# Second-layer gate logits with stationary weights in column groups, and the clears of a row buffer issued earlier

## The chip, the cores and the metric

One NeuronCore of one Trainium2 chip. The time is that of one execution on the device, in microseconds (us): 507.88 us, median of 3 runs (507.73 to 507.91). The page and the trace come from one more execution under the profiler.

## The reference

An attention over 4 batches of 512 tokens with 32 state rows each (8 heads of 64) gives 2176 rows of 512 features. Two mixture-of-experts layers follow, each with 8 experts, one expert for each row:

```python
logits = x @ w_gate                      # [2176, 512] @ [512, 8], fp32
expert_idx = np.argmax(logits, axis=1)
gate_w = softmax(logits)[n, expert_idx]
h = np.maximum(x_e @ w1[e], 0.0)         # 512 -> 1024
out = gate_w * (h @ w2[e])               # 1024 -> 512
```

The first layer has a capacity for each expert, the second has none. The argmax needs the logits in full fp32, so their product runs as fp32 matmuls, which stand in the trace as two weight loads and two matmuls each.

## The kernel before

All stages are written into one program with an order laid out by hand; each engine runs its own instructions in that order.

**Attention and first routing.** Four slots, one for a batch, write the 2176 rows to `xrows` in DRAM (a row is 512 features and its gate weight, 513 floats). The route of a batch takes the argmax, counts rows for each expert, and writes the gate weights with small DMAs of SP (`route`, L667, L668). Then lists of row numbers are made for each expert (`enlist_batch`).

**Layers.** Rows of one expert are worked in groups of 512 (four tiles of 128, the "quad"), gathered by indirect DMAs of GpSimd (L580). `stage` runs one group and `tail` its end together with the beginning of the next. `m1_quad` (L1056) does the first product of a chunk of 128 hidden features, 12 matmuls of 128x512, then ACT makes the rounded ReLU `hTh` (L1064) and DVE the rest `hTl` (L1065). `m2_quad` (L1068) does the second product: four tiles, three matmuls each. `ORDER` interleaves them. After every 3 or 4 matmuls the program calls a `Part`, which counts events 0, 1, 2, ... of the stage: at an event number other work is placed, such as casts of weight chunks, turns of tiles and logits. Weights come as raw fp32 chunks of 512 KB over SP's queue (`wload`, L273); ACT casts the high part (L277, L1291) and GpSimd or DVE subtracts for the low part (L278, L1292). `tail` turns the next group's four gathered tiles (`x_quad`, L1036, by `turn`, L1029): four transposes on TensorE, an ACT cast and a DVE subtraction each, in banks `ph[0]`, `pyT`, `ph[1]`, `pyT`. Small remainders of experts run beside groups (`small`, `one`).

**Gate logits of layer 2.** The finished rows of a layer 1 group lie in `ysb`. During the next group (and during the first group of layer 2 for the last rows) `Logits` makes their logits: `turn` (L1116) transposes a tile into bank `pyT` and ACT copies it to `yT` or to the scratch `hs`; `product` (L1120) multiplies, with the turned tile as stationary weights and the 512x8 gate matrix `wg2p` moving, 8 columns; DVE copies the 128x8 result (L1124). Four, six and six tiles are done in this run's three groups that have logits. `TURNS` and `TURNS0` give the event of each turn and each product. When the last product is done, `behind` (L1142) goes on: argmax on DVE, one-hot counts on TensorE (L1157 to L1161), places, gates and the store of the rows into `yrows` by indirect DMAs (L1091).

**The row buffer.** `yrows`, the input of layer 2, is cleared by four DMAs from a row of zeros (`fills`, L706 to L711). They are a step in the background queue `bgq`: generators of which each event of the first group takes up to four steps (`tick`, L103; `TQ = 4`). The queue is filled at L1529, behind what is left of the route of batch 1. The first group's stage begins at about 83 us; the loads of the second group's weights are placed at its event 22 (`planned`, L1503) and issued when the number of groups is known.

Of the kernel before, what the change touches and what calls it, by code (L numbers as in the profile page):

```python
# [10 lines left out]
F32 = mybir.dt.float32  # L11
# [8 lines left out]
P = 128  # L20
B, H, S, D = 4, 8, 512, 64
NS = 32
DM = H * D
E = 8
# [39 lines left out]
PLANNED, READY, GET = ((22, 29), 35, 0)  # L64
QUICK = (4, 3)
GAP = 2
TURNS0 = ((0, 1), (1, 3), (4, 5), (5, 6), (6, 7), (7, 8))
ON = ((1, 1, 1, 1), (1, 1, 1, 1), (0, 1, 0, 1), (0, 0, 0), (1, 1, 1, 1))
TURNS = ((6, 7), (7, 8), (8, 10), (11, 12), (12, 13), (13, 14))
ALL = (ET.Pool, ET.Activation, ET.PE, ET.DVE, ET.SP)  # L70
WHY = "the value is a count worked out on the chip within these bounds"

# [2 lines left out]
def moe_kernel(ctx: ExitStack, tc: tile.TileContext, x, state, wg1, w1a, w2a, cap, wg2, w1b, w2b, out):  # L75
# [17 lines left out]
    def ctile(shape, dt, name):  # L93
        return cp.tile(shape, dt, name=name)
# [5 lines left out]
    bgq = deque()  # L100
# [14 lines left out]
    def named(name, g):  # L115
        yield from g
        done.add(name)
# [9 lines left out]
    def abreast(*gs):  # L127


        gs = [[g, -1] for g in gs]  # L130
        while gs:
            n = 0
            for s in list(gs):
                if s[1] == clock[0]:
                    continue
                n += 1
                try:
                    if next(s[0]) is PAUSE:
                        s[1] = clock[0]
                    else:  # L140
                        yield
                except StopIteration:
                    gs.remove(s)
            if not n:
                yield PAUSE
# [10 lines left out]
    SP.dma_start(out=wg1_sb, in_=wg1.rearrange("(c p) e -> p c e", p=P))  # L156
    wg1h = ctile([D, H, E], F32, "wg1h")
    SP.dma_start(out=wg1h, in_=wg1.rearrange("(h d) e -> d h e", d=D))
    wg2p = ctile([P, NC1, E], F32, "wg2p")
    cap_i = ctile([P, 2], I32, "cap_i")  # L160


    zb = ctile([P, 4 * P], BF16, "zb")
    DVE.memset(zb, 0.0)
    ident = ctile([P, P], F32, "ident")
# [461 lines left out]
    def route(b0, nb, then=(), quick=False):  # L627

        n, run = nb * (R + 1), runs_[0]
        lg = lgs[:, b0:b0 + nb].rearrange("p b r e -> p (b r) e")  # L630
        gt = gts[:, b0:b0 + nb].rearrange("p b r -> p (b r)")
        ohb = rtp.tile([P, nb, R + 1, E], BF16, tag="oh", name="oh")
        oh = ohb.rearrange("p b r e -> p (b r) e")
        mv = []
        yield from argmax_onehot(rtp, lg, n, smask[:, 0:nb].rearrange("p b r -> p (b r)"), oh, mv)
        m, v = mv
        cs = rtp.tile([P, nb, R, E], BF16, tag="cs", name="cs")
        rs = rtp.tile([P, nb, 2, E], BF16, tag="rs2", name="rs2")
        DVE.tensor_copy(rs[:, :, 1], ohb[:, :, R])
        DVE.tensor_copy(cs[:, :, 1], ohb[:, :, 0])  # L640
        yield
        for r in range(2, R):
            DVE.tensor_tensor(out=cs[:, :, r], in0=cs[:, :, r - 1], in1=ohb[:, :, r - 1], op=ALU.add)
            yield
        DVE.tensor_tensor(out=rs[:, :, 0], in0=cs[:, :, R - 1], in1=ohb[:, :, R - 1], op=ALU.add)
        yield
        yield from pauses(QUICK[0]) if quick else idle(IDLE[0])
        w = nb * 2 * E
        rsv = rs.rearrange("p b a e -> p (b a e)")
        PE.matmul(pyv[:, 0:w], upper, rsv, start=True, stop=True)  # L650
        PE.matmul(pyv[:, w:2 * w], ones, rsv, start=True, stop=True)
        prs = rtp.tile([P, 2, nb, 2, E], F32, tag="prs", name="prs")
        DVE.tensor_copy(prs.rearrange("p t b a e -> p (t b a e)"), pyv[:, 0:2 * w])
        yield
        preb = rtp.tile([P, nb, R + 1, E], F32, tag="pre", name="pre")
        pre = preb.rearrange("p b r e -> p (b r) e")
        for i in range(nb):
            for a, r in ((0, 0), (1, R)):
                DVE.tensor_tensor(out=preb[:, i, r], in0=run, in1=prs[:, 0, i, a], op=ALU.add)
                DVE.tensor_tensor(out=run, in0=run, in1=prs[:, 1, i, a], op=ALU.add)  # L660
                yield
        yield from then

        def gates():
            yield from gate_of(rtp, lg, m, n, gt)
            for b in range(b0, b0 + nb):
                SP.dma_start(out=xrows[b * ST:b * ST + S, DM:ROW].rearrange("(p r) o -> p r o", p=P), in_=gts[:, b, 0:R, None])  # L667
                SP.dma_start(out=xrows[b * ST + S:(b + 1) * ST, DM:ROW], in_=gts[0:NS, b, R:R + 1])  # L668

        res = []  # L670

        def places():
            DVE.tensor_tensor(out=preb[:, :, 1:R], in0=cs[:, :, 1:R], in1=bc(preb[:, :, 0:1], [P, nb, R - 1, E]), op=ALU.add)
            yield
            far = rtp.tile([P, n, E], F32, tag="far", name="far")
            DVE.tensor_tensor(out=far, in0=pre, in1=bc(cape[:, None, :], [P, n, E]), op=ALU.is_ge)
            yield
            DVE.scalar_tensor_tensor(out=pre, in0=far, scalar=FAR, in1=pre, op0=ALU.mult, op1=ALU.add)
            yield
            yield from slots(rtp, oh, v, pre, n, res)  # L680

        yield from abreast(places(), gates())
        for i in range(nb):
            pp_[b0 + i] = [t[:, i * (R + 1):(i + 1) * (R + 1)] for t in res]
# [3 lines left out]
    def enlist_batch(b, quick=False, eng=(DVE, DVE, POOL)):  # L688

        pp, ek = pp_[b]  # L690
        todo = []
        for r in range(R + 1):
            np_ = P if r < R else NS
            oc = lsp.tile([P, NK], BF16, tag="loc", name="loc")
            ov = lsp.tile([P, 2, P], BF16, tag="lov", name="lov")
            yield from enlist(oc, ov, eng, np_, pp[:, r:r + 1], ek[:, r:r + 1], tida[:, b, r:r + 1], tidb[:, b, r:r + 1], todo)
            if len(todo) > LAG[b]:
                enlist_mm(*todo.pop(0))
        yield from pauses(QUICK[1]) if quick else idle(IDLE[1])
        while todo:  # L700
            enlist_mm(*todo.pop(0))
            yield from () if quick else idle(IDLE[2])
# [3 lines left out]
    def fills(*parts):  # L706

        g = NTOK // P
        for i in parts:
            lo, hi = g * i // 4, g * (i + 1) // 4  # L710
            SP.dma_start(out=yrows.rearrange("(g p) w -> p g w", p=P)[:, lo:hi], in_=bc(zeros[:, None, :], [P, hi - lo, ROW]))  # L711
        yield
# [16 lines left out]
    with ExitStack() as ac:  # L729
# [13 lines left out]
        xload(1, 2)  # L743
        xload(2, 2)
        SP.dma_start(out=cap_i, in_=bc(cap.bitcast(I32).rearrange("(o c) -> o c", o=1), [P, 2]))
        SP.dma_start(out=wg2p, in_=wg2.rearrange("(c p) e -> p c e", p=P))

        sd = ap_.tile([P, B, NH, P], F32, name="sd")
        vg = ap_.tile([P, B, NH, GW], F32, name="vg")
# [259 lines left out]
    hTh = wk2.tile([P, 2, QT * P], F32R, name="hTh")  # L1009
    hTl = wk2.tile([P, 2, QT * P], F32R, name="hTl")  # L1010
    hTf = wk2.tile([P, NC2, P], F32, name="hTf")
    hs = wk2.tile([P, 512], F32, name="hs")
    yT = [wk2.tile([P, NC1, P], F32, name="yT"), hs.rearrange("p (c t) -> p c t", c=NC1)]
    gq = [wk2.tile([P, QT], F32, name=f"gq{i}") for i in range(3)]
    g1 = wk2.tile([P, 1], F32, name="g1")
    gy = wk2.tile([P, QT + 2], F32, name="gy")
# [12 lines left out]
    def turn(bank, src):  # L1029

        for c in range(NC1):
            PE.transpose(bank[:, c * P:(c + 1) * P], src[:, c * P:(c + 1) * P], ident)
        return bank.rearrange("p (c t) -> p c t", c=NC1)
# [76 lines left out]
    class Logits:  # L1110

        def __init__(self, n, y0):
            self.n, self.y0, self.done = n, y0, 0
            self.lg = Sized(n).tile([P, n, E], F32, "lg", "lg2")

        def turn(self, i):  # L1116
            if i < self.n:
                ACT.copy(yT[i % 2].rearrange("p c t -> p (c t)"), turn(pyv, ysb[:, self.y0 + i]).rearrange("p c t -> p (c t)"))

        def product(self, i, bank):  # L1120
            if i < self.n:
                for c in range(NC1):
                    PE.matmul(bank[:, 0:E], yT[i % 2][:, c], wg2p[:, c], start=(c == 0), stop=(c == NC1 - 1))
                DVE.tensor_copy(self.lg[:, i], bank[:, 0:E])  # L1124
                self.done += 1

        def events(self, turns):

            ev = []
            for i, (t, p) in enumerate(turns):  # L1130
                c = (p + 2) // 7
                bank = ph[(c + 1) % 2] if (p + 2) % 7 < 4 else pyv
                ev += [(p, lambda i=i, bank=bank: self.product(i, bank)), (t, lambda i=i: self.turn(i))]
            return ev

        def alone(self):
            for i in range(self.n):
                self.turn(i)
                self.product(i, pyv)
            return self  # L1140

# [384 lines left out]
    POOL.memset(meta, 0.0)  # L1526
    POOL.memset(ysb[:, 0], 0.0)
    POOL.memset(ysb[:, NY - 2:NY], 0.0)
    bgq += [abreast(route(2, 2, (), True), enlist_batch(1, True)), fills(0, 1, 2, 3), abreast(plan_runs(rp, 0), named("lists", chain(enlist_batch(2, True), enlist_batch(3, True)))), plan_lists(rp, 0)]  # L1529
    for t in range(QT):  # L1530
        x_quad(t, ysb[:, 1 + t], py[t], gq[0])
    st = stage(0, 0, [(PLANNED[0], lambda: planned(0)), (READY, room)], TQ)
# [53 lines left out]
```

## Time and profile before

| | us |
|---|---|
| median of 3 runs (range) | 507.88 (507.73 to 507.91) |
| profiled execution, its own time | 511.39 |
| span in the trace, first to last instruction | 509.5 |
| TensorE busy | 445.8 (87%) |
| TensorE weight loads busy | 326.0 (64%) |
| VectorE (DVE) busy | 195.2 (38%) |
| ScalarE (ACT) busy | 165.9 (33%) |
| GpSimd (POOL) busy | 216.5 (42%) |
| mean granted TensorE clock | 0.948 |

Busy times are of the profiled execution. [...] In rows of the timeline the first two numbers are start and duration in us, then engine, line, operation, output and inputs, shapes and count; in brackets stands how long the engine was idle before and what released it. "PEld" is the weight loading of TensorE, "SPq" the DMA issuing of SP. Matmuls overlap, so the distance from one start to the next says more than a duration.

### The profile page before, as it was taken

The numbers are of one execution on the slowest core, as the hardware profiler recorded it, in microseconds if no ns is written. First come the engines' busy times: TensorE is split into PE (matmuls) and PEld (weight loads), VectorE is DVE, ScalarE is ACT, GpSimd is POOL, SyncE is SP. The second block draws the span as 40 slices with busy tenths as digits, with TensorE's granted clock in tenths as the row PEclk, the third lists the DMA queues.
The fourth block names the chain that finished last, engine by engine and source line by source line (L and its number), as shares of the span: only waits on it lengthen the run. The fifth ranks groups of instructions, "written<-read, shape, count | busy, mean of one in ns | idle before, by whom it ended". The sixth has DMA issues, their size and how long they took to land. (4 is left out here: it accounts for less than half of the span.)

```text
span 509.5 us, 7964 instructions
## 1 busy us (share of the span) xinstructions
PE 445.8 (87%) x2629; PEld 326.0 (64%) x2629; DVE 195.2 (38%) x666; ACT 165.9 (33%) x288; POOL 216.5 (42%) x197
## 2 busy tenths in 40 slices
PE   8969586979879989999997959999999999999940
PEld 5647365757664775676874748778745847668830
DVE  7967757895040161041264041584410100411110
ACT  4647434210143412345311334312431213451010
POOL 6432742564413445415446403357553506774030
PEclk9999878988979999999999988999999999999995
DMA  8264757079989996909633100025997848200020
GB/s 244 72 151 117 206 135 202 1 175 182 316 305 364 371 381 196 366 24 346 251 132 122 43 11 4 0 95 193 376 388 267 318 171 279 94 28 1 3 93 3
DMA packets 47364, 89.49 MB, mean 176 GB/s; under 512 B 8592, under 2 KB 21136, under 8 KB 47248
## 3 DMA queue, kind: packets, MB, share of 16 engines
q1 hardware_dynamic: 42128, 72.43, 44.5%
q0 software_dynamic: 5120, 15.76, 9.0%
q8 instruction: 43, 0.70, 0.6%
q14 instruction: 73, 0.60, 0.4%
HBM read 67.70 MB, written 21.52 MB: 175 GB/s over the span
## 5 line engine op out<-in xcount | busy, mean ns | idle before, releaser
L1065 DVE SCALAR_TENSOR_TENSOR hTl<-ph,hTh 128x512 fp32r<-128x512 f32 x48 | 33.2, 691 | 206.3 <-ACT hTh L1064 194.8
L1073 PE MATMUL py<-w1h,hTh 128*128 128x512 f32 x192 | 82.6, 430 | 0.0
L1073 PE MATMUL py<-w1l,hTh 128*128 128x512 f32 x192 | 76.4, 398 | 0.0
L1073 PE MATMUL py<-w1h,hTl 128*128 128x512 f32 x192 | 76.4, 398 | 0.0
L278 POOL TENSOR_TENSOR w1l<-raw,w1h 128x1024 fp32r<-128x1024 f32 x22 | 52.6, 2395 | 53.3 <-ACT w1h L277 53.2
L1292 POOL TENSOR_TENSOR w0l<-raw,w0h 128x512 fp32r<-128x512 f32 x40 | 51.0, 1287 | 56.0 <-ACT w0h L1291 51.2
L1064 ACT ACTIVATE hTh<-ph 128x512 fp32r<-128x512 f32 x48 | 28.7, 597 | 127.3 <-PE ph L1062 89.2
L1062 PE MATMUL ph<-xTh,w0h 128*128 128x512 f32 x192 | 54.4, 406 | 7.4 <-issue 5.5
L1062 PE MATMUL ph<-xTl,w0h 128*128 128x512 f32 x192 | 57.2, 421 | 0.0
L1062 PE MATMUL ph<-xTh,w0l 128*128 128x512 f32 x192 | 55.5, 411 | 0.3 <-issue 0.3
L1062 PEld LDWEIGHTS ph<-xTh,w0h 128*128 128x128 f32 x192 | 36.3, 193 | 16.4 <-issue 8.8
L1062 PEld LDWEIGHTS ph<-xTl,w0h 128*128 128x128 f32 x192 | 36.0, 194 | 13.4 <-issue 6.6
L1073 PEld LDWEIGHTS py<-w1h,hTh 128*128 128x128 f32 x192 | 37.1, 193 | 9.5 <-issue 3.4
L1073 PEld LDWEIGHTS py<-w1h,hTl 128*128 128x128 f32 x192 | 36.9, 192 | 8.3
L1073 PEld LDWEIGHTS py<-w1l,hTh 128*128 128x128 f32 x192 | 37.2, 194 | 7.0 <-issue 1.0
L1062 PEld LDWEIGHTS ph<-xTh,w0l 128*128 128x128 f32 x192 | 35.3, 192 | 9.9 <-issue 3.4
L1091 POOL DMA_INDIRECT out_dram<-ysb,dsti x15 | 14.9, 993 | 60.2 <-ACT ysb L1081 52.1
L1291 ACT CAST w0h<-raw 128x512 fp32r<-128x512 f32 x40 | 24.0, 618 | 22.1 <-DMA raw<-in_moe_w_dram 20.8
L1091 POOL DMA_INDIRECT yrows<-ysb,dsti x16 | 15.9, 996 | 29.6 <-DVE oc L336 8.4
L277 ACT CAST w1h<-raw 128x1024 fp32r<-128x1024 f32 x24 | 25.1, 1045 | 5.9 <-issue 5.9
L340 POOL TENSOR_SCALAR lov<-iofb,rpp,tidb 128x128 bf16<-128x128 bf16 (+1 forms) x20 | 16.6, 838 | 15.0 <-DVE rek L330 15.0
L880 PE MATMUL pav<-vg,e1T 128*128 128x264 f32 x56 | 18.0, 450 | 1.2 <-ACT xr L881 1.2
(325 smaller groups left out, 646.5 us busy)
## 6 DMA issues: line engine op xcount, KB each, us to landing
raw<-in_moe_w_dram SPq DMA_DIRECT2D x104, 512.0 KB
out_dram<-zb SPq DMA_DIRECT2D x2, 2176.0 KB
xrows<-xr SPq DMA_DIRECT2D x16, 256.0 KB
yrows<-zeros SPq DMA_DIRECT2D x3, 1026.0 KB
xb<-in_x_dram SPq DMA_DIRECT2D x6, 512.0 KB
yrows<-zeros SPq DMA_DIRECT2D x1, 1282.5 KB
xb<-in_x_dram SPq DMA_DIRECT2D x4, 256.0 KB
st<-in_state_dram SPq DMA_DIRECT2D x1, 256.0 KB
```

The lines of the kernel that those rows point to most:

```text
L277: ACT.copy(h, t)
L278: (POOL if on[c] else DVE).tensor_tensor(out=l, in0=t, in1=h.bitcast(F32), op=ALU.subtract)
L340: eng[2].tensor_scalar(ov[0:np_, 1], iofb[0:np_], pp[0:np_], tb[0:np_], op0=ALU.is_equal, op1=ALU.mult)
L880: PE.matmul(pv[:, a, 0:GW], e1_[b][:, r % 2, a, r // 2], vg[:, b, a], start=True, stop=True)
L1062: PE.matmul(p, w[k][:, 0, c * P:(c + 1) * P], u[:, k], start=(i == 0 and k == 0), stop=(i == 2 and k == NC1 - 1))
L1064: ACT.activation(out=hTh[:, c % 2], in_=p, func=AF.Relu)
L1065: DVE.scalar_tensor_tensor(out=hTl[:, c % 2], in0=p, scalar=0.0, in1=hTh[:, c % 2].bitcast(F32), op0=ALU.max, op1=ALU.subtract)
L1073: PE.matmul(py[t], u[:, c % 2, t * P:(t + 1) * P], w[c // 2][:, c % 2], start=(c == 0 and i == 0), stop=(c == NC2 - 1 and i == 2))
L1091: i = POOL.indirect_dma_start(out=(yrows if L == 0 else out)[:, :], out_offset=bass.IndirectOffsetOnAxis(ap=dsti[:, y:y + 1], axis=0), in_ ...
L1291: ACT.copy(h, t)
L1292: (POOL if ON[half][c] else DVE).tensor_tensor(out=l, in0=t, in1=h.bitcast(F32), op=ALU.subtract)
```

## The change

The gate matrix is loaded into a buffer padded with zeros to 32 columns (`wg2q`) and becomes the stationary operand, in each of four groups of 32 columns of the array. The moving operand is the turned rows, 32 tokens of each of two tiles for a group, 64 columns. The result has the logits along partitions, so DVE turns it by 32x32 blocks into a token-wise array with a stride of 32. Turns come in pairs, one product for a pair. `hs` becomes the second half of `yT`. Apart from that, `fills` moves from the second to the first place of what is appended to the background queue.

```diff
-TURNS0 = ((0, 1), (1, 3), (4, 5), (5, 6), (6, 7), (7, 8))
+TURNS0 = ((0, 1, 2), (4, 5, 6), (6, 7, 8))
-TURNS = ((6, 7), (7, 8), (8, 10), (11, 12), (12, 13), (13, 14))
+TURNS = ((6, 7, 8), (8, 10, 12), (12, 13, 14))
...
-    wg2p = ctile([P, NC1, E], F32, "wg2p")
+    wg2q = ctile([P, NC1, NS], F32, "wg2q")
...
+    DVE.memset(wg2q, 0.0)
     zb = ctile([P, 4 * P], BF16, "zb")
     DVE.memset(zb, 0.0)
...
-        SP.dma_start(out=wg2p, in_=wg2.rearrange("(c p) e -> p c e", p=P))
+        SP.dma_start(out=wg2q[:, :, 0:E], in_=wg2.rearrange("(c p) e -> p c e", p=P))
...
-    hs = wk2.tile([P, 512], F32, name="hs")
-    yT = [wk2.tile([P, NC1, P], F32, name="yT"), hs.rearrange("p (c t) -> p c t", c=NC1)]
+    yT = wk2.tile([P, 2, NC1, P], F32, name="yT")
+    hs = yT[:, 1].rearrange("p c t -> p (c t)")
...
-            self.lg = Sized(n).tile([P, n, E], F32, "lg", "lg2")
+            self.lgt = Sized(n).tile([P, n, NS], F32, "lg", "lg2")
+            self.lg = self.lgt[:, :, 0:E]
...
         def product(self, i, bank):
-            if i < self.n:
-                for c in range(NC1):
-                    PE.matmul(bank[:, 0:E], yT[i % 2][:, c], wg2p[:, c], start=(c == 0), stop=(c == NC1 - 1))
-                DVE.tensor_copy(self.lg[:, i], bank[:, 0:E])
-                self.done += 1
+            m = min(2, self.n - i)
+            if m <= 0:
+                return
+            for c in range(NC1):
+                for b in range(P // NS):
+                    PE.matmul(bank[b * NS:(b + 1) * NS, 0:m * NS], wg2q[:, c], yT[:, 0:m, c, b * NS:(b + 1) * NS], start=(c == 0), stop=(c == NC1 - 1))
+            DVE.transpose(self.lgt[:, i:i + m].rearrange("p n e -> p (n e)"), bank[:, 0:m * NS])
+            self.done += m
...
-            for i, (t, p) in enumerate(turns):
+            for j, (*ts, p) in enumerate(turns):
                 c = (p + 2) // 7
                 bank = ph[(c + 1) % 2] if (p + 2) % 7 < 4 else pyv
-                ev += [(p, lambda i=i, bank=bank: self.product(i, bank)), (t, lambda i=i: self.turn(i))]
+                ev.append((p, lambda j=j, bank=bank: self.product(2 * j, bank)))
+                ev += [(t, lambda i=2 * j + k: self.turn(i)) for k, t in enumerate(ts)]
...
-    bgq += [abreast(route(2, 2, (), True), enlist_batch(1, True)), fills(0, 1, 2, 3), abreast(plan_runs(rp, 0), named("lists", chain(enlist_batch(2, True), enlist_batch(3, True)))), plan_lists(rp, 0)]
+    bgq += [fills(0, 1, 2, 3), abreast(route(2, 2, (), True), enlist_batch(1, True)), abreast(plan_runs(rp, 0), named("lists", chain(enlist_batch(2, True), enlist_batch(3, True)))), plan_lists(rp, 0)]
```

`alone`, for rows without a group beside them, is changed to pairs in the same way.

## Rows read from the trace of the kernel before

**Rows 1.** Windows: us, busy us (count) of PE, PEld, DVE, ACT, POOL; PEclk; DMA share; GB/s.

```profile
225.00:250.00 25.00, 24.45 (x165) 17.13 (x163) 3.65 (x12) 11.32 (x20) 10.84 (x7) 1.00 0.83 298
...
90.00:95.00 5.00, 5.00 (x24) 4.04 (x22) 4.65 (x12) 1.53 (x2) 5.00 (x5) 1.00 0.00 0
...
105.00:110.00 5.00, 3.62 (x18) 2.74 (x17) 5.00 (x19) 0.26 (x1) 4.89 (x5) 1.00 0.81 213
...
140.00:145.00 5.00, 2.15 (x10) 1.64 (x9) 2.01 (x5) 2.20 (x5) 2.55 (x2) 0.77 0.81 285
145.00:150.00 5.00, 5.00 (x16) 3.96 (x15) 2.02 (x6) 1.74 (x3) 0.00 (x0) 0.54 0.77 272
```

**Rows 2.** Timeline of SP's DMA issues, 60 to 140 us.

```profile
86.99 0.61 SPq L668 DMA_DIRECT2D xrows<-gts  x1
102.90 0.52 SPq L667 DMA_DIRECT2D xrows<-gts  x1
...
105.47 3.46 SPq L711 DMA_DIRECT2D yrows<-zeros  x4
115.78 24.01 SPq L273 DMA_DIRECT2D raw<-in_moe_w_dram  x7
```

**Rows 3.** Timeline of ACT, 113 to 152 us.

```profile
133.36 0.62 ACT L1291 CAST w0h<-raw 128x512 fp32r<-128x512 f32 x1 [7.99 <-DMA raw<-in_moe_w_dram]
...
142.35 0.59 ACT L1064 ACTIVATE hTh<-ph 128x512 fp32r<-128x512 f32 x1
```

**Rows 4.** Timeline of PE, 113 to 152 us.

```profile
136.22 0.39 PE L1073 MATMUL py<-w1h,hTl 128*128 128x512 f32 x1
138.05 0.66 PE L1032 MATMUL ph<-ident,xg 128*128 128x128 f32 x4 [1.44 <-DMA xg<-xrows,rows]
...
143.72 1.11 PE L1032 MATMUL ph<-ident,xg 128*128 128x128 f32 x4 [2.85 <-DVE hTl L1065]
...
150.59 0.39 PE L1073 MATMUL py<-w1h,hTl 128*128 128x512 f32 x1
```

**Rows 5.** Timeline of POOL, 113 to 152 us: the first gather of the next group.

```profile
126.45 1.00 POOL L580 DMA_INDIRECT xg<-xrows,rows  x1 [0.30 <-issue]
```

**Rows 6.** Timeline of PE, end of the last layer 1 group.

```profile
293.30 0.40 PE L1073 MATMUL py<-w1h,hTl 128*128 128x512 f32 x1
...
299.92 0.39 PE L1073 MATMUL py<-w1h,hTl 128*128 128x512 f32 x1
```

**Rows 7.** Timeline of PE: a product of one tile without a wait, and the next matmul.

```profile
244.13 0.95 PE L1123 MATMUL pyT<-wg2p,yT 128*128 128x8 f32 x8
244.94 1.17 PE L1062 MATMUL ph<-xTh,w0l 128*128 128x512 f32 x4
```

**Rows 8.** Timeline of PE in the attention: the state read, before and after it.

```profile
20.77 1.16 PE L880 MATMUL pav<-vg,e1T 128*128 128x264 f32 x4
21.86 1.10 PE L889 MATMUL pt<-xb,e2n 128*32 128x64 f32 x64
22.89 1.16 PE L880 MATMUL pav<-vg,e1T 128*128 128x264 f32 x4
23.88 0.60 PE L796 MATMUL pt<-ident,xb 128*128 128x128 f32 x4
```

**Rows 9.** Who waited for the copies of L1118 (us, times); one such wait in PEld's timeline.

```profile
  PEld ph L1123: 4.7, 12
...
241.11 0.97 PEld L1123 LDWEIGHTS ph<-wg2p,hs 128*128 128x128 f32 x8 [0.47 <-ACT hs L1118]
```

**Rows 10.** The instructions of L827: ns min/median/max, first and last start us.

```profile
L827 DVE STREAM_TRANSPOSE u<-psT x8: 675/707/710, 11.1 to 49.2; 128x512 f32<-128x512 f32 x8
```

**Rows 11.** Timeline of PE: the one-hot counts after the four tiles' logits.

```profile
182.04 0.18 PE L1157 MATMUL pyT<-oh,upper 128*128 128x32 bf16 x1 [1.36 <-DVE oh L296]
```

**Rows 12.** Timeline of DVE at the start.

```profile
0.85 0.27 DVE L164 MEMSET zb<- 128x256 uint32 x1 [0.85 <-PEq L1563]
```

**Rows 13.** The instructions of L889: ns min/median/max, first and last start us.

```profile
L889 PEld LDWEIGHTS pt<-xb,e2n x256: 106/110/177, 21.9 to 73.0; 128*32 128x32 f32 x128
```

More of the change, by code (lines that the diff above doesn't have):

```diff
@@ L1113, in __init__ @@
             self.n, self.y0, self.done = n, y0, 0
-            self.lg = Sized(n).tile([P, n, E], F32, "lg", "lg2")
+            self.lgt = Sized(n).tile([P, n, NS], F32, "lg", "lg2")
+            self.lg = self.lgt[:, :, 0:E]
         def turn(self, i):
             if i < self.n:
-                ACT.copy(yT[i % 2].rearrange("p c t -> p (c t)"), turn(pyv, ysb[:, self.y0 + i]).rearrange("p c t -> p (c t)"))
+                ACT.copy(yT[:, i % 2].rearrange("p c t -> p (c t)"), turn(pyv, ysb[:, self.y0 + i]).rearrange("p c t -> p (c t)"))
         def product(self, i, bank):
-            if i < self.n:
-                for c in range(NC1):
-                    PE.matmul(bank[:, 0:E], yT[i % 2][:, c], wg2p[:, c], start=(c == 0), stop=(c == NC1 - 1))
-                DVE.tensor_copy(self.lg[:, i], bank[:, 0:E])
-                self.done += 1
+            m = min(2, self.n - i)
[6 more added lines that the diff above has]
+            self.done += m
         def events(self, turns):
             ev = []
-            for i, (t, p) in enumerate(turns):
+            for j, (*ts, p) in enumerate(turns):
                 c = (p + 2) // 7
                 bank = ph[(c + 1) % 2] if (p + 2) % 7 < 4 else pyv
-                ev += [(p, lambda i=i, bank=bank: self.product(i, bank)), (t, lambda i=i: self.turn(i))]
+                ev.append((p, lambda j=j, bank=bank: self.product(2 * j, bank)))
+                ev += [(t, lambda i=2 * j + k: self.turn(i)) for k, t in enumerate(ts)]
             return ev
         def alone(self):
-            for i in range(self.n):
+            for i in range(0, self.n, 2):
                 self.turn(i)
+                if i + 1 < self.n:
+                    self.turn(i + 1)
                 self.product(i, pyv)
```

## The prediction, made before the change was run

> **What bounds the kernel now.** I read the windows first. In the stretch of layer 1 where the second layer's gate logits are made, TensorE (PE) is busy 24.45 of 25 us at full clock [rows 1]: a microsecond taken from PE's stream there is a microsecond of the kernel. [...] And from 90 to 95 us the DMA engines move nothing, while from 105 us on they are full [rows 1]. So one transfer lies idle, then everything comes at once.
>
> SP's queue says what. It issues the gates of batch 1 until 87.6 us, has nothing until 102.9, and issues the four clears of yrows at 105.47, in 3.46 us. The weights of the next group follow at 115.78 [rows 2]. The clears are 2176 rows of 513 floats, 4.47 MB; at the 213 GB/s of the window they last some 21 us, to about 127. The weights go on the same queue behind them. ACT shows the price: the first of four casts of a new weight chunk starts at 133.36 after 7.99 us of waiting for that load, and the ReLU hTh behind the fourth starts only at 142.35 [rows 3]. PE cannot turn the third gathered tile before that bank is read: the first turn starts at 138.05, the third at 143.72, and the group's last matmul at 150.59 [rows 4]. The profile puts the first wait down to the gather and the second to DVE's hTl; hTl stands behind hTh, and hTh behind the cast.
>
> **The change, part by part.**
>
> *The clears move from behind the route of batches 2 and 3 to its front.* They go after the gates of batch 1 in SP's program, thus at about 87.6 us, into an idle queue; 21 us later, near 109, they are done, before the weights are issued. Four DMAs pass four small gate writes of SP (those of batches 2 and 3, issued from 102.90 on); these wait behind the clears until about 109 and are needed by the gathers issued from 126.45 on [rows 5], so 17 us cover them. POOL's queue is not passed. One background tick moves, which shifts the route by a quarter of an event, or by a whole one (about 1 us) where a pause rounds it up; the loads now have 11 us in hand, which hides it. What PE gains: before, from the start of the last matmul ahead of the four turns, 136.22, to that of the group's last matmul, 150.59, it took 14.37 us. The same stretch of the last layer 1 group, without waits and at full clock, runs from 293.30 to 299.92, 6.62 us [rows 6]. Difference 7.75 us, half-clock time included. Bounds: 0 (if the clears were not the cause) and 7.75; I take 7.75: the first weight chunk came 7 us after the clears' end near 127, so in an empty queue it comes 7 us after its issue, near 123 instead of 133. A loss is excluded as far as the bytes and the queue are the same and nobody needs the clears before the first rows of layer 2 are stored, a whole group later.
>
> *The products.* Before, each tile costs PE eight instructions with a 128-column weight load; where nothing waits, the next matmul starts 244.94 - 244.13 = 0.81 us later [rows 7]. Sixteen tiles (4, 6 and 6 in the three groups that have a product): 16 x 0.81 = 12.96 us. After, each pair costs 4 chunks x 4 column groups x 2 passes = 32 instructions, 128x32 weights and 64 moving columns. That is the very shape of the state read: 64 of them start at 21.86 and the next matmul at 22.89, 1.03 us [rows 8], so 32 take 0.52 if all scales. The four matmuls ahead of them take 1.09 where the four after them take 0.99, so entering costs 0.10; leaving I put at a few hundredths. I take 0.65, between 0.52 and 1.13. Eight pairs: 5.2 us. Gain 7.76 us.
>
> Those rows give 16 ns per instruction. [...]
>
> *The waits beside them.* Now PE waits 12 times, 4.7 us in all, mostly 0.47 us, for ACT's copy of the turned tile [rows 9]. After, both turns of a pair use the bank pyT: the second turn must wait for the first copy and the product for the second, wherever only three m2 matmuls lie between. That holds for five of the eight pairs (turns at 6 and 7, or 12 and 13): 5 x 0.85 = 4.25 us. Gain 0.45. If more spacing hid half of that it would be 2.1 more.
>
> *The DVE part.* Two copies per pair become one 32x32 block transpose of 128x64. The trace has it at 128x512 from PSUM, 0.71 us [rows 10]; extra price between 0 and 0.71 for the three transposes that something waits for (the last of each group); I take 0.1 each, 0.3 us, nearer the copy, since it is an eighth of the columns. The others lie in DVE's idle time before the next product.
>
> *What is late next.* The routing behind the last product runs on DVE, and PE already waits 1.36 us for its one-hot rows [rows 11]. The shorter last product is eaten there: 0.5 us back over three groups.
>
> *Small edits.* The 128x128 clear of the padded weights goes ahead of zb's clear on DVE, for which PE's first matmuls wait; zb's takes 0.27 us [rows 12], the new one between 0 and that: 0.15. The load of the padded weights waits for it, 8 us later: nothing. lg with a stride of 32: as many elements, nothing.
>
> **Sum.** -7.75 - 7.76 - 0.45 + 0.3 + 0.5 + 0.15 = -15.0 us. The profiled execution took 511.39 us, 3.5 above the median of the three runs, so it would come to 496.4, and the median 507.88 to **492.9**.
>
> **Rivals.**
> *The gathers set the tail, not the weights.* The first gather is issued at 126.45 [rows 5] and PE takes its tile at 138.05; the weights keep the DMA engines just as full then. For it: the first wait names the gather. Against: the 4.47 MB in front are gone. If the first tile still comes at 138.05, 1.6 us stay; tiles issued 1.3 us apart cost 0.4 more; with the clock falling again, as after the waits at 140 to 145, another 2.3 (5 us at 0.54 [rows 1]): 4.3 in all, 497.2. [...] No row here separates the queues.
> *The pair costs twice what I take,* 1.3 us: 5.2 lost, 498.1.
> *The clears don't move the tail:* SP is held, or the casts wait for something else. 500.7. Against: SP's empty stretch.
> *Slower: the column groups take turns.* If each instruction paid its own weight load, 0.110 us [rows 13], a pair would cost 3.52 us, eight 28.2 instead of 5.2: 15.0 saved turn into 8 lost, 515.9. It decides from 79 ns per instruction on (2.53 us a pair, where the sum is zero). Against: 64 such loads started within 1.03 us [rows 8].
>
> **How the numbers follow.** Forecast 0.72, gathers 0.13, pair twice as dear 0.05, clears without effect 0.06, groups in turn 0.04. The predicted time is the forecast's own. Low end: 0.52 per pair (-1.0), no DVE, clear and routing costs (-0.95) and half of the pair waits hidden (-2.1) give 488.9, so 489. The high end, 500, holds the gathers and the dear pair, and leaves out the last two cases. A measurement here tells about 0.2%, 1 us, from no change. Every case but the last is faster by more: faster 0.94, same 0.02 (a mix of no gain from the clears and dear pairs), slower 0.04.
>
> **What would show it.** Right: the clears issued near 88 us and windows from 88 to 109 at some 200 GB/s; no wait of ACT on a weight load near 133; PE's turns after group 0 without gaps and clock 1.0 there; 32 instructions of a product followed by the next matmul after 0.5 to 0.8 us; PE waiting about 0.4 us at second turns and products. Wrong: turns still waiting for gathered tiles at full DMA; products over 1 us; the wait before the one-hot matmuls grown by more than 0.5 us; a new idle stretch of PE where the earlier group meets a weight load.

## The result, and the profile after the change

Four executions of the changed kernel took 490.10 to 498.68 us, median 493.64; four of the kernel before 504.62 to 507.91, median 507.81. The ratio is 0.9713, interval 0.963 to 0.9795; every ratio here compares the means of those executions that lie within 1.5% of the fastest of their kernel, while medians and ranges are of all. Predicted were 492.9 us, 489 to 500. The profiled execution is the longest of the four: 498.68 us, span 496.8, against 511.39 and 509.5 before, which is also longer than any of the four there. Line numbers have moved on by 1 (L1091 is L1092) to 10 (L1157 is L1167).

Windows of the changed kernel, columns as in [rows 1]:

```profile
90.00:95.00 5.00, 4.63 (x27) 3.55 (x26) 4.90 (x15) 0.49 (x1) 4.37 (x4) 1.00 1.06 246
105.00:110.00 5.00, 2.94 (x16) 1.79 (x14) 4.96 (x23) 0.00 (x0) 3.49 (x3) 1.00 0.84 113
...
130.00:135.00 5.00, 5.00 (x29) 4.13 (x28) 2.20 (x5) 2.22 (x4) 1.50 (x2) 1.00 1.03 399
135.00:140.00 5.00, 5.00 (x27) 4.15 (x26) 3.12 (x10) 2.27 (x5) 0.00 (x0) 1.00 1.05 382
```

The empty DMA window at 90 us is full: in stretches of 5 us from 88 to 108 us the DMA engines move 266, 234, 225 and 168 GB/s, from 108 to 113 only 7, so the clears are done about when foreseen. PE's end of group 0 is busy at full clock (1.00 in both windows; the granted clock is a share of full speed) where [rows 1] had 2.15 of 5 us and clocks of 0.77 and 0.54. SP's queue, against [rows 2], and ACT's timeline, against [rows 3]:

```profile
86.66 0.61 SPq L669 DMA_DIRECT2D xrows<-gts  x1
87.37 3.47 SPq L712 DMA_DIRECT2D yrows<-zeros  x4
101.26 0.53 SPq L668 DMA_DIRECT2D xrows<-gts  x1
...
112.30 18.05 SPq L274 DMA_DIRECT2D raw<-in_moe_w_dram  x16
```

```profile
121.91 0.62 ACT L1301 CAST w0h<-raw 128x512 fp32r<-128x512 f32 x1 [1.49 <-DMA raw<-in_moe_w_dram]
125.63 0.60 ACT L1065 ACTIVATE hTh<-ph 128x512 fp32r<-128x512 f32 x1 [3.10 <-PE ph L1063]
126.12 1.65 ACT L1301 CAST w0h<-raw 128x512 fp32r<-128x512 f32 x3
131.18 0.60 ACT L1065 ACTIVATE hTh<-ph 128x512 fp32r<-128x512 f32 x1 [3.40 <-issue]
```

The clears go out 18 us earlier, the casts wait 1.49 us instead of 7.99, and hTh no longer stands behind them. Timeline of PE: the end of group 0 (against [rows 4, 6]), a product (against [rows 7]), the one-hot counts ([rows 11]), the beginning of layer 2, and a list matmul there:

```profile
131.40 0.40 PE L1074 MATMUL py<-w1h,hTl 128*128 128x512 f32 x1
131.63 0.60 PE L1033 MATMUL ph<-ident,xg 128*128 128x128 f32 x4
...
135.05 0.60 PE L1033 MATMUL pyT<-ident,xg 128*128 128x128 f32 x4
...
138.03 0.40 PE L1074 MATMUL py<-w1h,hTl 128*128 128x512 f32 x1
...
167.42 0.18 PE L1167 MATMUL pyT<-oh,upper 128*128 128x32 bf16 x1 [1.51 <-DVE oh L297]
...
225.88 0.65 PE L1130 MATMUL ph<-yT,wg2q 128*32 128x64 f32 x32
226.47 0.66 PE L1033 MATMUL pyT<-ident,ysb 128*128 128x128 f32 x4
...
281.26 0.39 PE L1074 MATMUL py<-w1h,hTl 128*128 128x512 f32 x1
287.31 0.79 PE L1063 MATMUL ph<-xTh,w0h 128*128 128x512 f32 x1 [5.66 <-issue]
290.59 1.44 PE L1063 MATMUL ph<-xTh,w0h 128*128 128x512 f32 x3 [2.49 <-issue]
...
327.29 0.59 PE L347 MATMUL listp<-ov,oc 128*96 128x256 bf16 x2 [5.14 <-DVE ov L341]
```

From 131.40 to 138.03 the end of group 0 takes 6.63 us, against 14.37 before and 6.62 foreseen. A pair's product takes 226.47 - 225.88 = 0.59 us. Two stops are new: 2.49 us after a single matmul of layer 2 (the stop of 5.66 us ahead of that matmul took 5.16 before), and 5.14 us at a list matmul. What the list matmul waited for stands in the timelines of DVE and POOL:

```profile
321.55 0.31 DVE L339 TENSOR_SCALAR ov<-iofb,rpp,meta 128x128 bf16<-128x128 bf16 x1
321.77 5.46 DVE L341 TENSOR_SCALAR ov<-iofb,rpp,meta 128x128 bf16<-128x128 bf16 x1
```

```profile
321.54 0.97 POOL L1092 DMA_INDIRECT yrows<-ysb,dsti  x1 [3.08 <-PE ph L1063]
322.53 4.64 POOL L279 TENSOR_TENSOR w1l<-raw,w1h 128x1024 fp32r<-128x1024 f32 x2
```

An operation of DVE that elsewhere takes 0.30 us ends 0.06 us after GpSimd has finished a store and two casts. It ends neither with the store, at 322.51, nor with the first of the casts: its 5.46 us run over three GpSimd instructions in a row. That DVE waits for GpSimd is the reading that fits; by what one holds up the other is in no row.

To see where the time went, I divided both executions at the starts of the same PE instructions. A plan is marked by its list matmul `pyT<-mk,la`, a one-hot by the first one-hot count of its group, and a logit turn is a turn of `ysb` (differences of starts, us):

| from, to | before | after | change |
|---|---|---|---|
| start, layer 1's plan | 123.09 | 118.15 | -4.94 |
| plan, first logit turn (group 1) | 43.97 | 36.36 | -7.61 |
| first logit turn, one-hot (group 1) | 14.98 | 12.91 | -2.07 |
| one-hot, first logit turn (group 2) | 55.46 | 55.74 | +0.28 |
| first logit turn, one-hot (group 2) | 19.01 | 15.58 | -3.43 |
| one-hot, first matmul of layer 2 | 48.96 | 48.57 | -0.39 |
| that matmul, first logit turn (layer 2) | 1.87 | 4.51 | +2.64 |
| first logit turn, one-hot (layer 2) | 20.95 | 17.49 | -3.46 |
| one-hot, layer 2's plan | 15.06 | 20.92 | +5.86 |
| plan, last matmul | 146.25 | 147.12 | +0.87 |

The sum is -12.25 us. The second line is the clears, the three logit lines the products, 8.96 us together. Of these three lines the first two repeat within 0.2 us in the other profiles with the same products, but the one in layer 2 runs from 17.45 to 18.86 us there, so its 3.46 holds some chance. The first line is no part of the change: most of it is the granted clock, which was 0.70 and 0.62 in the two windows from 110 to 120 us before and 1.00 after. In the fourteen profiles of this study that plan's matmul starts between 118.15 and 124.32 us, with and without each part of the change.

### The profile page after: what moved, and what is told of

Its sections match the earlier page's. It is cut to its first block, busy times and chain, and to the rows that moved or that the text cites. A ratio compares the mean times of both kernels' runs of the same rounds, so it can differ in the third digit from the quotient of the medians.

```text
span 496.8 us, 8205 instructions
## 1 busy us (share of the span) xinstructions
PE 433.9 (87%) x2757; PEld 314.3 (63%) x2757; DVE 199.3 (40%) x659; ACT 165.7 (33%) x288; POOL 217.1 (44%) x197
## 5 line engine op out<-in xcount | busy, mean ns | idle before, releaser
L1063 PE MATMUL ph<-xTh,w0h 128*128 128x512 f32 x192 | 55.9, 412 | 10.0 <-issue 8.4
L1063 PE MATMUL ph<-xTl,w0h 128*128 128x512 f32 x192 | 55.7, 411 | 0.0
L1063 PEld LDWEIGHTS ph<-xTl,w0h 128*128 128x128 f32 x192 | 35.0, 188 | 13.5 <-issue 6.4
L1092 POOL DMA_INDIRECT out_dram<-ysb,dsti x15 | 14.9, 993 | 63.6 <-ACT ysb L1082 52.7
L1092 POOL DMA_INDIRECT yrows<-ysb,dsti x16 | 15.9, 997 | 25.1 <-DVE oc L337 8.0
```

The costliest lines, as they stand in the source:

```text
L1063: PE.matmul(p, w[k][:, 0, c * P:(c + 1) * P], u[:, k], start=(i == 0 and k == 0), stop=(i == 2 and k == NC1 - 1))
L1092: i = POOL.indirect_dma_start(out=(yrows if L == 0 else out)[:, :], out_offset=bass.IndirectOffsetOnAxis(ap=dsti[:, y:y + 1], axis=0), in_ ...
```

## The experiments

They ran on three chips, four kernels on each; whether one of these is the chip of the first measurement is not known. The kernel before took 511.28 (504.59 to 519.11), 505.74 (501.22 to 511.59) and 508.09 us (501.54 to 514.07) there; ratios are to it on the same chip.

**e1_clears**: the kernel before, with the clears first and nothing else.

```diff
-    bgq += [abreast(route(2, 2, (), True), enlist_batch(1, True)), fills(0, 1, 2, 3), ...
+    bgq += [fills(0, 1, 2, 3), abreast(route(2, 2, (), True), enlist_batch(1, True)), ...
```

> The clears moved to the front, the logits as before. Theory (the clears held up the weight chunks, the chunks held up ACT's casts, the casts held up the turns of group 1): the tail of group 0 loses its waits, first turn to last matmul takes some 6.6 us instead of 14.4, and the kernel gains 7.7 to 12 us: 496 to 500 us. Rival (gathers set the tail): turns still wait some 2 us for xg, gain 3 to 6 us. Rival (the clears have no effect, all comes from the logits): within 1 us of before.

509.79 us, ratio 1.0008 (0.9964 to 1.0053). The stretch from plan to first logit turn is 36.22 us, as short as after the full change; yet no time is gained: the waits went as the theory had it, the time as the second rival. In the profile the gain is lost again between group 2's one-hot and layer 2's first matmul, a stretch of 56.22 us instead of 48.96. A part of that stands in DVE's and in POOL's timeline:

```profile
260.34 2.90 DVE L421 TENSOR_SCALAR elm<-kt,efk 96x8 f32<-96x8 f32 x1
```

```profile
259.86 0.97 POOL L1091 DMA_INDIRECT yrows<-ysb,dsti  x1 [2.18 <-PE listp L346]
260.85 2.36 POOL L278 TENSOR_TENSOR w1l<-raw,w1h 128x1024 fp32r<-128x1024 f32 x1
```

The same pattern: DVE's operand of the early list ends with the cast, and PE's matmul L427 waits 3.79 us instead of the 1.11 before. Then the granted clock is 0.64 and 0.68 from 260 to 270 us and 0.66 from 275 to 280, where it was 1.00 before; the four matmuls of L1062 at 264.56 take 2.08 us, in the kernel before (270.34) 1.20. How much of the lost clock follows from the wait is not shown.

**e2_logits**: the changed kernel with the clears back in their old place (the same diff, reversed).

> The new logits with the clears where they were. Theory: products of 0.58 us a pair instead of 1.62, second turns and products waiting 0.4 us as in the changed kernel; 2.1, 3.4 and 3.5 us less in the three groups, 9 us in all, of which the start of layer 2 may give back up to 8 (a blocked DVE operation of 5 us before the last list matmul and a longer code load, as in the profile of the changed kernel): 499 to 507 us. The tail of group 0 keeps its waits (first turn to last matmul above 13 us). Rival (the clears are the whole gain): 507 to 508.

506.67 us, ratio 0.9906 (0.9839 to 0.9974), 4.8 us of 511.28. Its logit stretches are 12.90, 15.59 and 18.85 us; its second stop at layer 2 costs 4.61 - 1.87 = 2.74. Against the 14.98, 19.01 and 20.95 of before that makes -2.1 - 3.4 - 2.1 + 2.7 = -4.9 us. That the two figures agree is partly chance: the profiled execution, 500.73 us, lies 6 us below the median. Against expectation the four turns at the end of group 0 did not wait as before: 133.43 to 137.48, 4.05 us instead of 7.86.

**e3_after** and **e4_late**: the changed kernel again; and with the last two casts of layer 2's first group behind its list matmuls.

```diff
+LATE2 = (0, 8, 26, 27)
-        lists = [at(SPLIT2, lambda c: wsplit(1, c, ON[4 if L or k else 2])), ev]
+        lists = [at(LATE2 if L and not k else SPLIT2, lambda c: wsplit(1, c, ON[4 if L or k else 2])), ev]
```

> The changed kernel once more. Theory: its times fall into two kinds, about 490 to 492 where DVE makes the last list operands of the first layer 2 group before GpSimd starts its two casts, and 495 to 499 where GpSimd is first and DVE waits some 5 us. Rival (the spread is the granted clock alone): no blocked DVE operation in a slow profile, or one in a fast profile too.

> The changed kernel with the last two casts of the second weights of layer 2's first group placed behind its list matmuls (events 26 and 27 instead of 14 and 20). Theory (GpSimd's casts block the last DVE list operation): no DVE list operation above 1 us there, no PE wait of 5 us before the last list matmul, the spread of the times shrinks to about 3 us and the median comes to 489 to 492. Rival (clock alone): median and spread as the changed kernel in the same call, 490 to 499. Second rival (the casts are then late for the products that use them, or DVE's work behind them is blocked instead): 492 to 496 with a new wait some 10 us later.

e3_after took 506.22 us, 496.35 to 513.26, ratio 0.9849 (0.9741 to 0.9956): faster than before, by less than in the first measurement. The list operand was held up again, for 5.47 us, and one-hot to plan took 20.94 us. The times do not fall into the two kinds foreseen. In e4_late that stretch takes 14.87 us; 501.64 us, five of six executions within 500.07 to 503.00, ratio 0.9875 (0.9821 to 0.9929). The small spread was foreseen, the median of 489 to 492 was not met. In both profiles with the long operand it ends 0.06 us after the second cast, so the casts are what it waits for, as far as a trace can tell. In the five profiles with the late places the casts start 0.6 to 1.1 us after the store, because they wait for ACT, and no operand is held up, not even in e6_cand, where it starts 0.18 us behind the store. That the late places remove the stop is likely, not shown: three of five profiles with the old places lack it too. The intervals of the two ratios overlap; the gain in time is not shown by this pair.

**e5_before**: a second profile of the kernel before.

> The kernel before once more, unchanged, for a second profile of it. Theory A (the price of the late clears depends on how far the transfer of the second layer's weights has come when group 0's hidden state is needed, so it differs from execution to execution): the first to the last of the four turns of group 0's hidden state takes clearly less than the 7.86 us of the first profile, 3.6 to 6 us, as the 4.05 us of e2_logits, which has the same late clears. Theory B (the price is fixed by the bytes of the clears): 7.9 us again, within 0.5.

503.36 us. Timeline of ACT, to be held against [rows 3], and the turns in PE's timeline, against [rows 4]:

```profile
129.09 0.62 ACT L1291 CAST w0h<-raw 128x512 fp32r<-128x512 f32 x1 [4.59 <-issue]
...
135.52 0.62 ACT L1291 CAST w0h<-raw 128x512 fp32r<-128x512 f32 x1 [1.91 <-DMA raw<-in_moe_w_dram]
136.04 0.59 ACT L1064 ACTIVATE hTh<-ph 128x512 fp32r<-128x512 f32 x1
```

```profile
135.59 0.60 PE L1032 MATMUL ph<-ident,xg 128*128 128x128 f32 x4
...
139.00 0.60 PE L1032 MATMUL pyT<-ident,xg 128*128 128x128 f32 x4
```

The clears are as late, at 104.59, but from 125 to 130 us the DMA engines moved 325 GB/s where the first profile had 175; the casts began 4.3 us earlier and ended just ahead of need, and the four turns take 3.41 us, like after the change. B falls, and A holds in kind: the turns take a little less than its 3.6 to 6 us. The stretch from plan to first logit turn is 37.76 us, in the first profile 43.97, with early clears 36.2 to 36.4 in all ten profiles. Late clears cost 1.4 us here and 7.6 there. Whether the execution or the chip sets that stays open, since the first measurement has only one profile with late clears.

**e6_cand**: e4_late, and the last second-matrix cast of group 2 on DVE.

```diff
+        on = (1, 1, 1, 0) if k == 2 and not L else ON[4 if L or k else 2]
-        ... wsplit(1, c, ON[4 if L or k else 2])), ev]
+        ... wsplit(1, c, on)), ev]
```

> The changed kernel with the last two casts of layer 2's first group behind the list matmuls (as in e4_late) and the last second-matrix cast of layer 1's group 2 on VectorE instead of GpSimd. Theory (GpSimd casts hold VectorE's list operands up): in the trace no VectorE operation of either list takes over 1 us, layer 2's one-hot to its plan takes 15 us (against 20.9 in e3_after), group 2's early list starts 0 to 3 us after its operands, and the time is 8 to 14 us below the kernel before on the same chip (ratio 0.972 to 0.984) with a spread of runs under 6 us. Rival (TensorE's half-clock stretches, not the casts, make the spread of e3_after): ratio 0.982 to 0.99 and a spread of over 10 us as there.

498.81 us, 494.53 to 500.00, ratio 0.9849 (0.9792 to 0.9907): spread and stretches are as the theory says (5.5 us; 14.85 us from one-hot to plan; the early list's wait 1.11), while the ratio lies in the rival's range, just outside the theory's. The second stop of layer 2 is there still.

**e9_pad**: e6_cand and four small matmuls near the program's start.

```diff
         warm(WARM3)
+        for _ in range(4):
+            PE.matmul(pyv[:, 0:8], zb[:, 0:P], zb[:, 0:8], start=True, stop=True)
```

> e6_cand with four more matmuls of 8 columns on TensorE early in the program, where TensorE waits anyway: nothing else changes but that all later TensorE code stands a few instructions further on. Theory (the second stop, 2.5 us after the first matmul of layer 2, comes from where the code of the branch lies, since TensorE waits for nothing there): the stop goes away or moves to another instruction; if it goes away, layer 2's first matmul to its first logit turn takes 1.9 us instead of 4.5, and the time is 2 to 3 us below e6_cand. Rival (the stop is a wait for data or for a transfer): it stays at the same matmul with 2.5 us, and the time is that of e6_cand within 1 us.

492.77 us, 491.83 to 497.99, ratio 0.9777 (0.9713 to 0.9841). Timeline of PE in e6_cand, then in e9_pad:

```profile
293.63 0.52 PE L1064 MATMUL ph<-xTh,w0h 128*128 128x512 f32 x1 [4.72 <-issue]
297.12 1.44 PE L1064 MATMUL ph<-xTh,w0h 128*128 128x512 f32 x3 [2.98 <-issue]
298.36 1.06 PE L1034 MATMUL pyT<-ident,ysb 128*128 128x128 f32 x4
```

```profile
290.17 2.08 PE L1066 MATMUL ph<-xTh,w0h 128*128 128x512 f32 x4 [5.42 <-issue]
292.04 1.05 PE L1036 MATMUL pyT<-ident,ysb 128*128 128x128 f32 x4
```

The stop is gone, with no datum or transfer changed. It is there in all seven profiles that have the new logits without the four matmuls, and in none of the three with them. That the place of the code decides is the reading that fits; the place itself is in no row. The DMA view of the changed kernel from 287.4 to 290.5 us, inside its second stop, shows what the engines did there:

```profile
q8 instruction: 1, 0.02, 2.5%
q14 instruction: 2, 0.02, 1.6%
```

No data, only packets of instructions. Such a packet of 16 KB on q8 starts 0.6 us after layer 2's first matmul here, and 0.9 and 0.7 us after it in before and e9_pad, where there is no second stop, so the packet alone does not make it; that PE needs what it brings only in some of them is argued, and the trace does not name the reader of a queue. Of the 6.0 us between the medians (2 to 3 were foreseen) the stop explains 2.9. In the profiles 3.7 us lie before 80 us, where the two kernels differ only in the four matmuls and the granted clock fell below 1.00 from 30 to 80 us in e6_cand, only from 60 to 70 in e9_pad: chance, as far as two profiles tell.

**e8_clears2**: e1_clears with e6_cand's cast on DVE.

> e1_clears (the kernel before with the clears first, its logits unchanged) with the last second-matrix cast of layer 1's group 2 on VectorE instead of GpSimd. Theory (the 8.8 us that the early clears had gained by group 2's one-hot were taken back there by the cast that held VectorE's early list up): the wait of the list's matmul is 1 to 2 us instead of 3.79, and the time is 4 to 8 us below the kernel before (ratio 0.984 to 0.992). Rival (the clears were worth little in the executions of that chip to begin with, the first profile being the exception): ratio 0.995 to 1.003 whatever the list waits.

502.62 us, ratio 0.9934 (0.9891 to 0.9978). The early list's matmul (L427, at 261.21) waits 1.10 us instead of 3.79, and the stretch from group 2's one-hot to layer 2 takes 48.22 us. Neither range holds the ratio: both theories were half right. The two edits together are worth some 3 us, not 8. That the clears alone gained nothing because of the held operand fits, but e1_clears ran on another chip and the two intervals overlap.

**e7_order**: the loops of the product swapped, so that eight matmuls in a row go to one column group.

```diff
-            for c in range(NC1):
-                for b in range(P // NS):
+            for b in range(P // NS):
+                for c in range(NC1):
```

> The changed kernel with the two loops of the logits' product swapped, so that eight matmuls in a row go to the same column group (the changed kernel goes round the four groups). Theory (matmuls of neighbouring column groups run side by side, and that is why a pair takes 0.58 us): a pair takes 0.9 us at least, from 32 matmuls of 64 columns at the 0.227 us that 512 columns take, and up to 1.7 us if each has to wait for its weights, as half of the 64 matmuls before did. Rival (the pair is bound by the issue of 32 instructions, at 18 ns each, whatever their groups): 0.58 us again, within 0.05.

One execution, 507.57 us. Timeline of PE:

```profile
232.26 1.40 PE L1130 MATMUL ph<-yT,wg2q 128*32 128x64 f32 x32
233.59 0.66 PE L1033 MATMUL pyT<-ident,ysb 128*128 128x128 f32 x4
```

1.33 us instead of 0.59, with the same instructions: 42 ns each in place of 18. The rival falls and the theory's range holds: with neighbours in different column groups a pair takes 0.59 us, with neighbours in one 1.33. What the eight in a row wait for is not shown: they share the columns, and each also adds to the same 32 rows of the result.

**e10_best, e11_after, e12_lateclears**: e9_pad again, the changed kernel itself, and e9_pad with the clears in their old place, on one chip.

> e9_pad once more, word for word the same, beside the changed kernel itself on one chip. Theory (the second stop at layer 2's start and the held list operand are what the changed kernel lost of its gain): 2.5 us for the stop and 5 to 6 us for the list operand in those executions in which it is held: 3 to 8 us below the changed kernel's median, and runs within 6 us of each other. Rival (TensorE's half-clock stretches decide, and they fall by chance): no more than 2 us below it, with a spread as wide as the changed kernel's.

> The changed kernel itself on the same chip. Theory: its list operand in layer 2 takes over 5 us again behind the GpSimd casts, its second stop after the first matmul of layer 2 is 2.5 us again, and its median lies 3 to 8 us above e10_best. Rival: within 2 us of e10_best.

> e10_best with the clears back in their old place. Theory A (the clears cost time only in executions in which the second layer's weights come late, as in the first profile of the kernel before, and nothing in e5_before): group 0's four turns span 3.4 to 4.1 us in its profile, and its median is 0 to 3 us above e10_best. Theory B (late clears cost what the first profile of the kernel before shows): four turns over 7.9 us, the median 6 to 9 us above e10_best.

| | us | ratio to before |
|---|---|---|
| e10_best | 495.56 (493.00 to 496.69) | 0.9774 (0.9725 to 0.9824) |
| e11_after | 501.04 (499.01 to 503.33) | 0.9899 (0.9847 to 0.9951) |
| e12_lateclears | 499.35 (495.85 to 502.10) | 0.9864 (0.9806 to 0.9923) |

e10_best beats both kernels: by 5.5 us the changed one, within the 3 to 8 expected, and no execution of either falls among the other's. It has three edits beyond the changed kernel (the late casts, the cast of group 2 on DVE, the four matmuls), and the pair does not divide the gain among them; in the profiles, 4.1 us apart, the stop is 2.7. In e11_after's profile the second stop is 2.55 us, as expected, but the list operand was not held up (one-hot to plan 14.77 us), which the theory had wrong for this execution: DVE's operation began 0.14 us ahead of GpSimd's store. It was 0.23 and 0.34 us behind it in the two executions that were held up, and 0.14 and 0.15 behind in e2_logits and e7_order, which were not. Less than a tenth of a microsecond, between 0.15 and 0.23, divides the two kinds in these five profiles.

e12_lateclears lies 3.8 us above e10_best, between the two theories' ranges and nearer A's. Its four turns take 3.41 us. The rest shows in SP's timeline, first of e12_lateclears, then of e10_best:

```profile
105.37 3.50 SPq L713 DMA_DIRECT2D yrows<-zeros  x4
115.83 30.22 SPq L275 DMA_DIRECT2D raw<-in_moe_w_dram  x16
```

```profile
88.43 3.49 SPq L713 DMA_DIRECT2D yrows<-zeros  x4
...
113.85 18.40 SPq L275 DMA_DIRECT2D raw<-in_moe_w_dram  x16
```

Behind late clears the sixteen weight loads are issued over 30.22 us, else over 18.40, and the stretch from plan to first logit turn takes 38.40 us instead of 36.39; two groups of matmuls of a small remainder (`pyT<-raw,xTf`, L1234) wait 0.19 and 0.17 us there for such a load. The remaining 1.8 us of the median are within the spread. This pair, six executions each on one chip, is the cleanest price of the late clears: the means differ by 4.2 us, 95% interval 1.7 to 6.6.

The stretches of the table above, where the theories differ, in ten profiles (us):

| | plan to logits | logits, group 1 | group 2 | layer 2's start | one-hot to plan |
|---|---|---|---|---|---|
| before | 43.97 | 14.98 | 19.01 | 1.87 | 15.06 |
| e5_before | 37.76 | 14.98 | 19.00 | 1.88 | 15.00 |
| e1_clears | 36.22 | 14.98 | 19.01 | 1.87 | 15.79 |
| e2_logits | 38.42 | 12.90 | 15.59 | 4.61 | 14.88 |
| after | 36.36 | 12.91 | 15.58 | 4.51 | 20.92 |
| e3_after | 36.37 | 13.09 | 15.59 | 4.55 | 20.94 |
| e4_late | 36.36 | 12.90 | 15.59 | 4.53 | 14.87 |
| e7_order | 36.41 | 13.64 | 17.37 | 4.74 | 15.20 |
| e11_after | 36.37 | 12.91 | 15.58 | 4.58 | 14.77 |
| e10_best | 36.39 | 12.91 | 15.59 | 1.87 | 14.79 |

## Why the prediction was right, and where it was not

**The total** came within 1 us, 493.64 against 492.9, and part of that is luck. In the pair of profiles the two main terms, clears and products, gained 16.57 us, as the mechanism had it. Two losses that the prediction had not seen took back 8.50 (the second stop 2.64, the held list operand 5.86), and 4.94 us came on top by chance, from before the first plan, mostly granted clock. How many of the other three executions had these losses is not known. In two later measurements, e3_after and e11_after, the same kernel had ratios of 0.9849 and 0.9899, which on 507.81 us are 500.1 and 502.7, above the stated range. The first interval, 0.963 to 0.9795, does not meet e11_after's, 0.9847 to 0.9951: the first measurement was a favourable one, and why is open but for the clears below.

**The clears.** Foreseen 7.75 us; the pair of profiles shows 7.61, with the mechanism as told: clears in an idle queue, casts without their wait, hTh free, turns without gaps, and the first cast at 121.91 where 123 was foreseen. The weak step is the size taken for it, "Bounds: 0 (if the clears were not the cause) and 7.75; I take 7.75". The wait of [rows 3] belonged to a profile with slow transfers (175 GB/s from 125 to 130 us, where the three later profiles with late clears have 300 to 331). Those three give 1.4 to 2.0 us (37.76, 38.42, 38.40 less 36.4), and time says some 4 (e12_lateclears against e10_best). A smaller gain from the clears fits the ratios of 0.9849 and 0.9899 later on, but is not shown to be their cause. Whether every execution of the first measurement paid 7.6 us stays open: only one was profiled.

**The products.** 0.65 us a pair foreseen, 0.59 measured; the gain is 12.96 - 8 x 0.59 = 8.2 us instead of 7.8. The state read's shape was the right row to scale from. Going round the groups a matmul takes 18 ns, where that row gave 16, and 42 ns in e7_order.

**The waits beside them.** 4.25 us were foreseen instead of 4.7. The waits of PE's weight loads after the change (us in all, times, longest us):

```profile
PEld ph L1130 <- ACT yT L1120: 2.3, 5, 0.5
PEld pyT L1033 <- ACT yT L1120: 2.0, 5, 0.5
...
PEld pyT L1130 <- ACT yT L1120: 0.4, 1, 0.4
```

Five pairs with two waits each, as told, and one product more: 4.7 us, so nothing gained against [rows 9]. The miss is 0.45 us.

**DVE.** The block transpose of 128x64 takes 0.25 us. PE's waits before the one-hot counts of the three groups grew from 1.36, 0.34 and 0.57 us to 1.51, 0.30 and 0.89, 0.43 us in all, where 0.8 were put down for the transposes and for a shorter product being eaten there. The three logit stretches together gained 8.96 us where the terms gave 7.4; products and waits as measured make 7.8, and the other 1.1 us are open, with the chance in layer 2's stretch among them. The clear of the padded weights takes 0.17 us, 0.15 foreseen.

**Rivals.** The gathers do not set the tail: issued from 121.51, and PE's first turn at 131.63 waits for nothing. The dear pair (1.3 us) and the groups in turn fall with 0.59; with the loops the other way round the dear pair would have come true to the tenth (e7_order, 1.33). The clears move the tail.

**What was not seen.** "What is late next" looked at the routing and stopped there. Moving group 2 and layer 2 by some microseconds against GpSimd's queue lets a cast meet a list operand, in two of the five profiles that have the new logits and the casts in their old place, and with the new PE code a second stop of 2.5 us follows the first of 5 at layer 2's entry. The first could have been asked of the trace of before, in two places. An operand of the early list that takes 0.22 us at 268.80 took 1.98 us at 62.32, again until a cast had ended, and 1.97 or 1.98 us at 59 to 63 us in e1_clears, e2_logits, after, e3_after and e4_late. And at the place in question DVE's last list operand led GpSimd's store, with the two casts right behind it, by 0.78 us, so that anything that moves DVE against GpSimd by that much is a risk. DVE's and POOL's timelines of before:

```profile
62.32 1.98 DVE L421 TENSOR_SCALAR elm<-kt,efk 96x8 f32<-96x8 f32 x1
...
340.96 0.31 DVE L340 TENSOR_SCALAR ov<-iofb,rpp,meta 128x128 bf16<-128x128 bf16 x1
```

```profile
61.84 2.44 POOL L278 TENSOR_TENSOR w0l<-raw,w0h 128x1024 fp32r<-128x1024 f32 x1 [2.64 <-ACT w0h L277]
...
341.74 0.97 POOL L1091 DMA_INDIRECT yrows<-ysb,dsti  x1 [4.08 <-PE listp L346]
342.72 4.74 POOL L278 TENSOR_TENSOR w1l<-raw,w1h 128x1024 fp32r<-128x1024 f32 x2
```

The second could not be seen: before, there is one stop of 5.16 us.

## What to carry to other kernels

Small stationary tiles paid here with neighbours in the stream going to different column groups (0.59 us a pair; 1.33 with neighbours in one, 2 x 0.81 = 1.62 in the kernel before); go round the groups in the inner loop, and price a pair from a row of that shape. A wait on a transfer in one profile need not be there in the next (late clears cost 7.6 us in before, 1.4 in e5_before): before a gain is put at its whole length, take a second profile, and measure the result more than once, since the same kernel came out at 0.971, 0.985 and 0.990 of the one before. After moving anything, look for DVE operations that last as long as a GpSimd instruction beside them (5.46 us here in place of 0.30), and for "issue" stops a few instructions into a branch (2.49 us here); two casts moved behind the lists, one moved to DVE and four dummy matmuls were together worth 5.5 us here.

## What the runs showed of the hardware that was not expected

A DVE operation that elsewhere took 0.30 us took 5.46 us beside a store and two casts of GpSimd in a row, and ended 0.06 us after the second cast (after; 5.47 us in e3_after). It was held when it started 0.23 and 0.34 us behind the store, and not when it started 0.14 and 0.15 us behind (e2_logits, e7_order).

With the same instructions at layer 2's entry, four matmuls more or fewer early in the program make a stop of 2.5 to 3.0 us go or appear: 1.87 or 1.88 us from layer 2's first matmul to its first logit turn in the three profiles with them, 4.51 to 4.74 in the seven without. That the place of the code does it is the likely reading.

The same program's transfers ran at 175 GB/s in one profile and 325 in another (before and e5_before, 125 to 130 us), and the casts of the first weights began 4.3 us apart; the first measurement's chip may differ from e5_before's.
